# Attention tails transposed with all 128 rows, and the first batch's reciprocals taken from one column named 64 times

## The chip, the cores and the metric

The kernel runs on one core of a Trainium2 chip. The metric is device time in microseconds (us) of that core; lower is better. "Before" is the kernel as it stood, "after" the kernel with the change. The engines are TensorE (PE, with its weight loads shown apart as PEld), VectorE (DVE), ScalarE (ACT), GpSimd (POOL) and the DMA queues (SP and others).

## The reference

Attention with rotary positions feeds two dense blocks. Shapes: batch 4, 8 heads, 576 positions, head size 64; the model width is 512.

```python
def _attn_ref(q, k, v):                       # (4, 8, 576, 64) each
    ...
    q_rot, k_rot = (rotate(q), rotate(k))
    scores = scale * np.matmul(q_rot, k_rot.transpose(0, 1, 3, 2))
    scores = scores - np.max(scores, axis=-1, keepdims=True)
    attn = np.exp(scores)
    attn = attn / (np.sum(attn, axis=-1, keepdims=True) + 1e-09)
    return np.matmul(attn, v).astype(np.float32)

def reference(**kwargs):
    ...
    x = _moe_ref(x=x, **moe_kwargs)           # token mix, relu squared, two products, sigmoid gate
    return _moe2_ref(x=x, **moe2_kwargs)      # relu, normalise, product over positions, gate, product
```

The change touches attention alone: how the matrix of exponentials P (`attn` before the division) is transposed for the product with `v`, and how the row's 1/sum reaches the place where it is multiplied in.

## The kernel before, in words

**Units.** Attention is cut into 72 units, 18 for each batch. Unit m handles 128 query rows of two heads at once, against all 576 keys. 576 is four times 128 and 64 over, so of every nine units the fifth (m mod 9 = 4) is a **tail**: it takes the 64 rows left over of four heads (two pairs). In a tail the rows 0 to 63 of every tile belong to one head of a pair and rows 64 to 127 to the other. The tails are m = 4, 13, 22, 31, 40, 49, 58 and 67; 4 and 13 lie in the first batch (m below 18).

**Steps of a unit**, by the names in the code. `scores` (PE, rows with tile `s`) makes two score tiles, one for each head (in a tail, one for each pair). `top` (DVE, L342) finds the row maxima, once for each score tile. `expo` (ACT, L347) writes P into tile `pf` and the row sums into `sm`; `total` (ACT, L351) adds 1e-9 and `norm` (DVE, L354) takes the reciprocal. `spread` (ACT, L358) copies each reciprocal 64 times wide into tile `rb`. `turn` n = 0, 1, 2 (PE, tile `t`) transposes P in three parts: n = 0 and 1 are four blocks of 128 keys each, n = 2 is the block of left-over keys together with the transposed reciprocals from `rb`. In a tail, `turn` 0 and 1 work on 64 rows at a time, eight blocks each, and `turn` 2 makes eight small products. `take` n (L395) copies the transposed part from PSUM to tile `pt`: n = 0 and 1 on ACT, n = 2 on DVE; in a tail every part goes to two `pt` tiles. `values` (PE, tile `v`, L402) multiplies `pt` with `v`; it follows units 1, 4, 6 and 8 of every nine. `gather` (DVE, L414) multiplies the result by the reciprocals, which stand in chunk 9 of `pt`. In the text t5_2 is part 2 of the turning of unit 5, s6 the scores of unit 6, top 6/0 and exp 6/0 the first of the two `top` and `expo` steps of unit 6.

**Filler.** In the first batch DVE, ACT and POOL also decode the weights (L156 to L174, three DVE steps to a piece: L156, L164, L165) and rotate the next q and k (products L249, sums L257). From unit 19 on PE has products of the finished batch to run between the units (`mk` L498, `mv` L537). After attention come the dense blocks of the second function.

**What sets the order.** A planner (class `Plan`, a list scheduler) is given every step with its engine, an estimated length, what it depends on and a rank, and writes out one fixed order for each engine; the engines then run in that order and wait on semaphores. So a step that is changed in length or in its dependencies can move other steps. The score tiles have two buffers (one unit's worth), so the scores of unit m+1 wait for the exponentials of unit m. The transposed parts have two PSUM slots.

## Time and profile before

| | us |
|---|---|
| median of 3 runs | 777.41 |
| lowest and highest | 776.02 and 779.28 |
| the profiled execution's own time | 777.82 |
| its span, first to last instruction | 776.0 |
| PE busy in the span | 740.8 |
| DVE, ACT busy | 481.0, 463.6 |

The profile is of one execution. A row of the timeline gives the start, the duration, the engine, the line, the operation and its tiles (written <- read), how many instructions were merged, and in brackets how long the engine had been idle and whose end released it. The form in front of the shapes, such as 64*128 or 128*64, is the part of PE's array that the instruction uses, rows by columns. PEld rows start when the weights are loaded. A matmul's own duration is longer than the distance to the next one, since they are pipelined; what a matmul costs a busy PE is the distance from start to start.

### The profile page before, as it was taken

The numbers are of one execution on the slowest core, as the hardware profiler recorded it, in microseconds if no ns is written. First come the engines' busy times: TensorE is split into PE (matmuls) and PEld (weight loads), VectorE is DVE, ScalarE is ACT, GpSimd is POOL, SyncE is SP. The second block draws the span as 40 slices with busy tenths as digits, with TensorE's granted clock in tenths as the row PEclk, the third lists the DMA queues.
The fourth block names the chain that finished last, engine by engine and source line by source line (L and its number), as shares of the span: only waits on it lengthen the run. The fifth ranks groups of instructions, "written<-read, shape, count | busy, mean of one in ns | idle before, by whom it ended". The sixth has DMA issues, their size and how long they took to land.

```text
span 776.0 us, 14283 instructions
## 1 busy us (share of the span) xinstructions
PE 740.8 (95%) x5696; PEld 649.9 (84%) x5696; DVE 481.0 (62%) x881; ACT 463.6 (60%) x1061; POOL 112.2 (14%) x132
## 2 busy tenths in 40 slices
PE   4788889999999999999999999999999999999997
PEld 2555569788888888888888898989989999998997
DVE  5988898888777877687856434246463342545111
ACT  3878898778777878778777644245333322533221
POOL 1432424011211211211111000002020000101000
PEclk9999999999999999999999999999999999999999
DMA  8363540542342442533232175072201212010101
GB/s 294 116 201 122 175 129 20 164 149 99 134 163 85 141 156 88 182 113 126 92 131 70 51 268 210 24 264 57 87 1 62 63 46 77 17 31 1 62 1 62
DMA packets 35268, 84.13 MB, mean 108 GB/s; under 512 B 4545, under 2 KB 10433, under 8 KB 35202
## 3 DMA queue, kind: packets, MB, share of 16 engines
q1 hardware_dynamic: 34658, 82.63, 31.6%
q8 instruction: 45, 0.74, 0.4%
q10 hardware_dynamic: 544, 0.59, 0.3%
q14 instruction: 21, 0.17, 0.1%
HBM read 60.65 MB, written 22.55 MB: 107 GB/s over the span
## 4 chain that ended last, share of the span: by engine, by line
PE 88%; DVE 4%; ACT 3%; DMA 3%; issue 0%; SPq 0%; ACTq 0%
PE mv L537 13%; PE mk L498 11%; PE v L402 11%; PE t L378 9%; PE sp L673 8%; PE r L673 7%; PE u L673 7%; PE hv L737 6%; PE o L673 6%; PE s L330 6%; PE s L338 3%; ACT pf L347 1%; DVE raw L249 1%; DMA wi<-wd 1%; PE s L327 1%; DVE sm L342 1%
## 5 line engine op out<-in xcount | busy, mean ns | idle before, releaser
L342 DVE TENSOR_REDUCE sm<-s 128x1 f32<-128x576 f32 x144 | 107.2, 751 | 36.9 <-PE s L330 30.5
L347 ACT ACTIVATE pf<-s,sm 128x576 f32<-128x576 f32 x144 | 107.0, 745 | 14.1 <-DVE sm L342 13.0
L537 PE MATMUL mv<-kh,wv 128*128 128x288 f32 x512 | 114.1, 305 | 1.2 <-ACT kh L512 1.2
L498 PE MATMUL mk<-x,wk 128*128 128x288 f32 x768 | 110.2, 298 | 0.4 <-ACT rl L505 0.4
L395 ACT COPY pt<-t 128x512 f32<-128x512 f32 (+1 forms) x160 | 84.8, 542 | 34.3 <-PE t L378 32.0
L498 PEld LDWEIGHTS mk<-x,wk 128*128 128x128 f32 x768 | 102.9, 188 | 0.7 <-ACT rl L505 0.6
L378 PE MATMUL t<-ident,pf 128*128 128x128 f32 x512 | 82.5, 284 | 14.0 <-ACT pf L347 14.0
L537 PEld LDWEIGHTS mv<-kh,wv 128*128 128x128 f32 x512 | 85.6, 191 | 5.4 <-issue 3.9
L378 PEld LDWEIGHTS t<-ident,pf 128*128 128x128 f32 x512 | 56.6, 141 | 39.9 <-issue 16.4
L402 PE MATMUL v<-pt,vt 128*64 128x256 f32 (+1 forms) x640 | 87.5, 411 | 0.0
L537 PE MATMUL mv<-kl,wv 128*128 128x288 f32 x256 | 76.5, 299 | 0.6 <-DVE kl L516 0.6
L402 PEld LDWEIGHTS v<-pt,vt 128*64 128x64 f32 x640 | 44.3, 136 | 31.7 <-issue 4.1
L673 PE MATMUL sp<-ws,vn 128*128 128x288 f32 x384 | 53.9, 295 | 0.0
L673 PE MATMUL r<-xr,wr 128*128 128x288 f32 x384 | 52.5, 296 | 1.2 <-ACT vs L543 1.2
L673 PE MATMUL o<-g,wo 128*128 128x288 f32 x384 | 52.9, 296 | 0.5 <-ACT os L796 0.5
L673 PEld LDWEIGHTS r<-xr,wr 128*128 128x128 f32 x384 | 51.7, 188 | 1.8 <-ACT vs L543 1.5
L673 PEld LDWEIGHTS sp<-ws,vn 128*128 128x128 f32 x384 | 52.4, 188 | 0.7
L673 PEld LDWEIGHTS o<-g,wo 128*128 128x128 f32 x384 | 51.7, 188 | 1.4 <-ACT os L796 1.2
L673 PE MATMUL u<-x,wi 128*128 128x288 f32 x384 | 52.0, 296 | 0.0
L673 PEld LDWEIGHTS u<-x,wi 128*128 128x128 f32 x384 | 51.6, 188 | 0.3
L537 PEld LDWEIGHTS mv<-kl,wv 128*128 128x128 f32 x256 | 48.9, 191 | 1.2 <-DVE kl L516 1.2
L249 DVE TENSOR_TENSOR raw<-raw,cst 128x1152 f32<-128x1152 f32 (+1 forms) x34 | 45.6, 1344 | 5.7 <-DMA raw<-kp 4.9
(347 smaller groups left out, 1200.3 us busy)
## 6 DMA issues: line engine op xcount, KB each, us to landing
raw<-kp SPq DMA_DIRECT2D x15, 576.0 KB, 3.8
raw<-qp SPq DMA_DIRECT2D x15, 576.0 KB, 4.3
vt<-vp SPq DMA_DIRECT2D x16, 320.0 KB, 3.8
xd<-xt SPq DMA_DIRECT2D x16, 288.5 KB, 3.2
vd<-vs SPq DMA_DIRECT2D x32, 144.0 KB, 1.8
v<-vd SPq DMA_DIRECT2D x16, 288.0 KB, 2.7
out<-os SPq DMA_DIRECT2D x15, 288.0 KB, 2.1
wi<-wd SPq DMA_DIRECT2D x8, 512.0 KB, 9.1
```

The costliest lines, as they stand in the source:

```text
L249: nc.vector.tensor_tensor(t["raw", k][:, :, z], t["raw", k][:, :, z], cst[:, :, z], op=ALU.mult)
L330: nc.tensor.matmul(ps[j][:, h, :HALF], t[a, 0][r, 128 * c:128 * c + 128], t[b, 1][r, x], **f)
L338: nc.tensor.matmul(o, q[r, 128 * c:min(128 * c + 128, S)], k[r, h * HALF:(h + 1) * HALF], start=True, stop=True)
L342: nc.vector.tensor_reduce(st["sm"][:, 0, j:j + 1], st["s"][j][:, :, :HALF], axis=AX.XY, op=ALU.max, negate=True)
L347: nc.scalar.activation(st["p"][:, j, :].rearrange("p (a b) -> p a b", a=2), st["s"][j][:, :, :HALF], AF.Exp, bias=st["sm"][:, 0, j:j + 1], ...
L378: nc.tensor.transpose(pt[:, c, :], p[:, n, k:k + 128], ident)
L395: nc.scalar.copy(o, x) if eng == "ACT" else nc.vector.tensor_copy(o, x)
L402: nc.tensor.matmul(pv[HEAD[j], z], v[:, 4 * j + c if c < 4 else 8 + j, :], pt[:, 4 * j + c if c < 4 else 8, z], start=c == 0, stop=c == 4)
L498: nc.tensor.matmul(ps[:, :HALF], wk[w][:, c, fc * 128:(fc + 1) * 128], a[:, c, :], start=k == 0, stop=k == 11)
L537: nc.tensor.matmul(xs["v", dc][:, :HALF], wv[w][:, fc, dc * 128:(dc + 1) * 128], a, start=k == 0, stop=k == 23)
L673: nc.tensor.matmul(ps[:, h, :HALF], w, a[:, h * HALF:(h + 1) * HALF], start=m == 0, stop=m == n - 1)
L737: nc.tensor.matmul(ps[:, :FS], x[a][:, d, c:c + 128], wi[w][:, d, FS:], start=k == 0, stop=k == 11)
```

## The change

Three things are changed.

1. A tail's `turn` 0 and 1 transpose all 128 rows at once: four blocks of 128 x 128 each, part 0 for the first pair and part 1 for the second (before, part 0 was the lower 64 rows of both pairs and part 1 the upper 64). Since the two heads' key blocks are offset by 64 keys, the second head's blocks have to be moved up or down by 64 partitions when they are copied. So `take` 0 and 1 of a tail are three copies each instead of two, `take` 2 six instead of two. `turn` 0 now waits for the first exponential alone. The order of chunks in `pt` is changed to fit (ends in chunk 4, second head in chunks 5 to 8).
2. `spread` is left out in the first batch and in all tails. There the reciprocals are turned by a product with the identity whose weights are one column of `sm` named 64 times (two products for a unit, four small ones in a tail). The other units keep the copy and the transpose.
3. The planner's estimates and dependencies for these steps are adapted.

```diff
@@ -360,39 +360,43 @@
         def turn(n, slot):
             pt = st["t", n] = ps_t.tile([128, 4, 128], F32, tag=f"t{slot}", name=f"t{m}_{n}")
             p = st["p"]
-            if tail and n < 2:
+            if tail and n == 2:
                 for u in range(2):
-                    for c in range(4):
-                        k = 64 * n + 128 * c
-                        nc.tensor.transpose(pt.rearrange("p c (h q) -> p (c h) q", h=2)[:, 4 * u + c, :],
-                                            p[HEAD[n], u, k:k + 128], ident[HEAD[n], HEAD[n]])
-            elif tail:
+                    nc.tensor.transpose(pt[0:64, u, :], p[:, u, 512:], ident)
                 for u in range(2):
-                    for k in range(2):
-                        for j, r in enumerate(HEAD):
-                            nc.tensor.matmul(pt[r, u, HEAD[k]], st["r"][r, u, :] if k else p[r, u, 512 - 512 * j:576 - 512 * j],
-                                             ident[r, r], start=True, stop=True)
+                    for j, r in enumerate(HEAD):
+                        nc.tensor.matmul(pt[r, 2 + u, 0:64], st["sm"][r, 3, u:u + 1].to_broadcast([64, 64]), ident[r, r], start=True, stop=True)
             elif n < 2:
                 for c in range(4):
-                    k = 64 * n + 128 * c
+                    k = (0 if tail else 64 * n) + 128 * c
                     nc.tensor.transpose(pt[:, c, :], p[:, n, k:k + 128], ident)
             else:
                 nc.tensor.transpose(pt[:, 0, :], p.rearrange("p a b -> p (a b)")[:, 512:640], ident)
-                nc.tensor.transpose(pt[:, 1, :], st["r"].rearrange("p a b -> p (a b)"), ident)
+                if m >= 18:
+                    nc.tensor.transpose(pt[:, 1, :], st["r"].rearrange("p a b -> p (a b)"), ident)
+                else:
+                    for j, r in enumerate(HEAD):
+                        nc.tensor.matmul(pt[r, 1, :], st["sm"][:, 3, j:j + 1].to_broadcast([128, 64]), ident, start=True, stop=True)
 
         def take(n, eng):
-            for u, d in enumerate(into):
+            for d in into if n == 2 else into[n if tail else 0:][:1]:
                 if "pt" not in d:
                     d["pt"] = at.tile([128, 10, 320], F32, tag=f"pt{d['n'] % PTB}", name=f"pt{d['n']}")
-                o = d["pt"][:, 4 * n:min(4 * n + 4, 10), 256:320]
-                if not tail:
-                    o, x = d["pt"][:, 4 * n:min(4 * n + 4, 10), 128 * part:128 * part + 128], st["t", n]
-                    x = x if n < 2 else x[:, 0:2, :]
-                elif n < 2:
-                    x = st["t", n].rearrange("p c (h q) -> p (c h) q", h=2)[:, 4 * u:4 * u + 4, :]
-                else:
-                    x = st["t", n][:, u, :].rearrange("p (h q) -> p h q", h=2)
-                nc.scalar.copy(o, x) if eng == "ACT" else nc.vector.tensor_copy(o, x)
+            copy = nc.scalar.copy if eng == "ACT" else nc.vector.tensor_copy
+            x, z, (lower, upper) = st["t", n], slice(256, 320), HEAD
+            if not tail:
+                o = into[0]["pt"][:, :, 128 * part:128 * part + 128]
+                copy(o[:, 5 * n:5 * n + 4, :] if n < 2 else o[:, 4:10:5, :], x if n < 2 else x[:, 0:2, :])
+            elif n < 2:
+                o = into[n]["pt"]
+                copy(o[:, 0:4, z], x[:, :, lower])
+                copy(o[upper, 4:8, z], x[lower, :, upper])
+                copy(o[lower, 5:9, z], x[upper, :, upper])
+            else:
+                for u, d in enumerate(into):
+                    copy(d["pt"][lower, 4, z], x[lower, u, lower])
+                    copy(d["pt"][upper, 8, z], x[lower, u, upper])
+                    copy(d["pt"][:, 9, z], x[:, 2 + u, 0:64])
 
         def values(slot):
             pv = duo["v"] = ps_m.tile([128, 512], F32, tag=f"m{slot}", name=f"v{m}")
@@ -400,7 +404,7 @@
             for c in range(5):
                 for j in range(2):
                     nc.tensor.matmul(pv[HEAD[j], z], v[:, 4 * j + c if c < 4 else 8 + j, :],
-                                     pt[:, 4 * j + c if c < 4 else 8, z], start=c == 0, stop=c == 4)
+                                     pt[:, 5 * j + c if c < 4 else 4, z], start=c == 0, stop=c == 4)
 
         def rows(i):
             if i not in xt:
@@ -427,15 +431,16 @@
                              m - 0.5)
         t = add("ACT", 0.2, total, [exps[m, 1]], m - 0.3)
         nm = add("DVE", 0.17, norm, [t], m - 0.3)
-        sp = add("ACT", 0.26, spread, [nm], m - 0.3)
-        ready = [[exps[m, 0], exps[m, 1]] if tail else [exps[m, 0]], [exps[m, 1]], [sp]]
+        sp = nm if tail or m < 18 else add("ACT", 0.3, spread, [nm], m - 0.3)
+        ready = [exps[m, 0], exps[m, 1], sp]
         for n in range(3):
-            turned[m, n] = add("PE", (0.5, 0.5, 0.8)[n] if tail else (0.44, 0.44, 0.22)[n], lambda slot, n=n: turn(n, slot),
-                               ready[n], m + 0.1 * n, take="t", kind="t")
+            turned[m, n] = add("PE", (0.44, 0.44, 0.75 if tail else 0.33 if m < 18 else 0.22)[n], lambda slot, n=n: turn(n, slot),
+                               [ready[n]], m + 0.1 * n, take="t", kind="t")
             eng = ("ACT", "ACT", "DVE")[n]
-            x = add(eng, ((0.68, 0.68, 0.55) if tail else (0.59, 0.59, 0.42))[n], lambda n=n, eng=eng: take(n, eng),
-                    [turned[m, n]] + [y for d in into for y in freed.get(d["n"] - PTB, [])], m - 0.2, give=turned[m, n])
-            for d in into:
+            to = into if n == 2 else into[n if tail else 0:][:1]
+            x = add(eng, (1.13, 1.13, 0.95)[n] if tail else (0.59, 0.59, 0.42)[n], lambda n=n, eng=eng: take(n, eng),
+                    [turned[m, n]] + [y for d in to for y in freed.get(d["n"] - PTB, [])], m - 0.2, give=turned[m, n])
+            for d in to:
                 d["ev"].append(x)
         if part and k != 3 or tail:
             v = add("PE", 2.9 if duo["cols"] > 256 else 2.3, values, duo["ev"] + [vloads[w[0][0]]], m + 0.9, take="m", kind="v")
```

Three places of the order. **DVE around units 5 and 6** (first batch). `raw` are the operands of the rotation, `rot` its result, `I-` pieces of weights, `xt` the attention's result. Before:

```order
L342 TENSOR_REDUCE sm5_380<-s11_379 128x1
L395 COPY pt1_290<-t4_2_405 128x2x64
L395 COPY pt2_386<-t4_2_405 128x2x64
L257 TENSOR_TENSOR rot2_1_437<-raw2_1_264 128x576
L354 RECIPROCAL sm5_380<-sm5_380 128x2
L249 TENSOR_TENSOR raw2_0_269<-raw2_0_269,cst_90 128x1152
L414 TENSOR_TENSOR xt0_276<-v4_426,pt1_290 128x320
L257 TENSOR_TENSOR rot2_0_466<-raw2_0_269 128x576
L342 TENSOR_REDUCE sm6_455<-s12_453 128x1
L395 COPY pt2_386<-t5_2_474 128x2x128
L342 TENSOR_REDUCE sm6_455<-s13_454 128x1
```

After:

```order
L249 TENSOR_TENSOR raw2_0_269<-raw2_0_269,cst_90 128x1152
L354 RECIPROCAL sm5_371<-sm5_371 128x2
L257 TENSOR_TENSOR rot2_0_432<-raw2_0_269 128x576
L156 TENSOR_SCALAR I-435_436<-I-307_308 128x512
L418 TENSOR_TENSOR xt0_276<-v4_414,pt1_288 128x320
L164 TENSOR_SCALAR I-307_308<-I-307_308 128x512
L165 SCALAR_TENSOR_TENSOR I-435_436<-I-435_436,I-307_308 128x512
L389 COPY pt2_392<-t5_2_468 128x2x128
L342 TENSOR_REDUCE sm6_452<-s12_450 128x1
L342 TENSOR_REDUCE sm6_452<-s13_451 128x1
```

The copy of t5_2 and a piece of weights (L156, L164, L165) now stand ahead of the first top of unit 6 (the copies of the tail, two before and six now, stand just ahead of these rows).

**DVE from unit 3 to unit 4** (unit 4 is the first tail). Before:

```order
L342 TENSOR_REDUCE sm3_285<-s7_284 128x1
L156 TENSOR_SCALAR I-311_312<-I-131_132 128x512
L164 TENSOR_SCALAR I-131_132<-I-131_132 128x512
L165 SCALAR_TENSOR_TENSOR I-311_312<-I-311_312,I-131_132 128x512
L234 TENSOR_SCALAR mix4_96<-mix4_96 128x4 x2
L354 RECIPROCAL sm3_285<-sm3_285 128x2
L342 TENSOR_REDUCE sm4_329<-s8_327 128x1
L395 COPY pt1_290<-t3_2_349 128x2x128
L342 TENSOR_REDUCE sm4_329<-s9_328 128x1
```

After:

```order
L342 TENSOR_REDUCE sm3_283<-s7_282 128x1
L156 TENSOR_SCALAR I-310_311<-I-131_132 128x512
L164 TENSOR_SCALAR I-131_132<-I-131_132 128x512
L165 SCALAR_TENSOR_TENSOR I-310_311<-I-310_311,I-131_132 128x512
L249 TENSOR_TENSOR raw2_1_265<-raw2_1_265,cst_90 128x1152
L354 RECIPROCAL sm3_283<-sm3_283 128x2
L342 TENSOR_REDUCE sm4_326<-s8_324 128x1
L389 COPY pt1_288<-t3_2_344 128x2x128
L342 TENSOR_REDUCE sm4_326<-s9_325 128x1
```

A product of the next rotation (L249) has come ahead of the reciprocal of unit 3 and the tops of unit 4, and the two small steps of L234 have left.

**PE, second half of the first tail** (unit 4) to the scores of unit 6 (s12 and s13 are its two score tiles). Before:

```order
L367 MATMUL t4_1_389<-ident_95,pf4_357 128x64 x8
L373 MATMUL t4_2_405<-ident_95,pf4_357 64x64 x2
L373 MATMUL t4_2_405<-ident_95,rb4_401 64x64 x2
L373 MATMUL t4_2_405<-ident_95,pf4_357 64x64 x2
L373 MATMUL t4_2_405<-ident_95,rb4_401 64x64 x2
L378 MATMUL t5_0_421<-ident_95,pf5_415 128x128 x4
L402 MATMUL v4_426<-pt1_290,vt0_134 64x320 x10
L338 MATMUL s12_453<-rot1_1_259,rot1_0_262 128x288
L338 MATMUL s13_454<-rot1_1_259,rot1_0_262 128x288
```

After:

```order
L372 MATMUL t4_1_382<-ident_95,pf4_351 128x128 x4
L365 MATMUL t4_2_396<-ident_95,pf4_351 64x128 x2
L368 MATMUL t4_2_396<-ident_95,sm4_326 64x64 x4
L406 MATMUL v4_414<-pt1_288,vt0_134 64x320 x10
L372 MATMUL t5_0_441<-ident_95,pf5_411 128x128 x4
L338 MATMUL s12_450<-rot1_1_260,rot1_0_263 128x288
L338 MATMUL s13_451<-rot1_1_260,rot1_0_263 128x288
```

The product v4 now comes ahead of t5_0, and the tail's parts are 128 rows deep. Around unit 13 the same happens to v13 and t14_0. Apart from these two places the units' steps on PE stand in the same order up to the first `mk`; of the fillers after it some have moved past a neighbour.

## Rows read from the trace of the kernel before

**Rows 1.** The page, part 2: PE's busy tenths in 40 slices of 19.4 us.

```profile
PE   4788889999999999999999999999999999999997
```

**Rows 2.** Busy time by stage: us, then PE, PEld, DVE, ACT, POOL busy (instructions), clock, DMA.

```profile
8.20:109.00 100.80, 82.28 (x583) 51.79 (x583) 89.27 (x163) 80.89 (x199) 33.30 (x27) 1.00 0.51 167
...
140.00:447.00 307.00, 307.00 (x2626) 263.52 (x2626) 230.88 (x432) 237.21 (x593) 46.01 (x42) 1.00 0.36 121
```

**Rows 3.** PE's waits from 8.2 to 109 us: whom for, total us, times, longest.

```profile
PE t L378 <- ACT pf L347: 14.0, 12, 1.8
...
PE t L381 <- ACT rb L358: 0.8, 1, 0.8
```

**Rows 4.** Groups by line, 8.2 to 109 us: count | busy, mean ns | idle before.

```profile
L358 ACT COPY rb<-sm 128x128 f32<-128x128 f32 x19 | 5.6, 296 | 2.0 <-DVE sm L354 2.0
...
L395 ACT COPY pt<-t 128x256 f32<-128x256 f32 x8 | 2.5, 376 | 0.0
...
L395 DVE COPY pt<-t 128x128 f32<-128x128 f32 x4 | 1.0, 280 | 0.0
```

**Rows 5.** Timeline of one regular pair of units (10 and 11) of the first batch.

```profile
60.70 1.24 PE L338 MATMUL s<-rot,rot 64*128 64x288 f32 x8
...
62.78 0.42 DVE L395 COPY pt<-t 128x256 f32<-128x256 f32 x1
63.05 0.75 ACT L347 ACTIVATE pf<-s,sm 128x576 f32<-128x576 f32 x1
...
64.52 1.50 PE L338 MATMUL s<-rot,rot 64*128 64x288 f32 x8
...
67.28 1.92 PEld L402 LDWEIGHTS v<-pt,vt 128*64 128x64 f32 x18 [0.34 <-ACT pt L395]
...
70.17 1.24 PE L338 MATMUL s<-rot,rot 64*128 64x288 f32 x8
```

**Rows 6.** Timeline around the first tail (unit 4).

```profile
29.34 1.64 DVE L165 SCALAR_TENSOR_TENSOR I-311_312<-I-311_312,I-131_132 128x512 int32<-128x512 int32 x1
...
31.13 0.73 DVE L342 TENSOR_REDUCE sm<-s 128x1 f32<-128x576 f32 x1
...
34.69 1.35 DVE L249 TENSOR_TENSOR raw<-raw,cst 128x1152 f32<-128x1152 f32 x1
...
37.78 0.65 PE L378 MATMUL t<-ident,pf 128*128 128x128 f32 x4 [0.72 <-ACT pf L347]
```

**Rows 7.** Timeline around the second tail (unit 13).

```profile
79.09 0.40 PE L367 MATMUL t<-ident,pf 64*128 64x64 f32 x3 [0.47 <-ACT pf L347]
...
80.40 0.69 DVE L165 SCALAR_TENSOR_TENSOR I-847_848<-I-847_848,I-567_568 128x512 int32<-128x512 int32 x1
...
82.69 0.66 PE L378 MATMUL t<-ident,pf 128*128 128x128 f32 x4 [0.74 <-ACT pf L347]
...
86.11 1.24 PE L338 MATMUL s<-rot,rot 64*128 64x288 f32 x8
```

**Rows 8.** Timeline of PEld while PE is full: scores and a turning between fillers.

```profile
200.02 0.19 PEld L537 LDWEIGHTS mv<-kh,wv 128*128 128x128 f32 x1
200.37 0.30 PEld L330 LDWEIGHTS s<-rh,rh 64*128 64x128 f32 x4 [0.16 <-issue]
...
200.88 0.32 PEld L330 LDWEIGHTS s<-rh,rl 64*128 64x128 f32 x4
201.37 0.42 PEld L378 LDWEIGHTS t<-ident,pf 128*128 128x128 f32 x4 [0.17 <-issue]
...
201.98 0.19 PEld L537 LDWEIGHTS mv<-kh,wv 128*128 128x128 f32 x1
```

**Rows 9.** The same for the end of a tail (unit 40).

```profile
247.62 0.51 PEld L367 LDWEIGHTS t<-ident,pf 64*128 64x128 f32 x7
248.20 0.19 PEld L373 LDWEIGHTS t<-ident,pf 64*64 64x64 f32 x4
...
248.54 0.20 PEld L373 LDWEIGHTS t<-ident,rb 64*64 64x64 f32 x4
```

## The prediction

> **What bounds the kernel now.** I read the utilisation by slices first: PE is at 9 tenths or more from about 140 us to the end and has holes only ahead of that [rows 1]. The stage table says how large they are: from 8.2 to 109 us PE is busy 82.3 of 100.8 us, DVE 89.3 and ACT 80.9, and no engine is full; from 140 to 447 us PE is busy all 307 us and DVE and ACT are not [rows 2]. So there are two different questions. In the first batch the time is a chain that runs around the engines, and only what lies on that chain counts. After 109 us, where PE has the fillers, only PE's own instructions and the gaps between them count.
>
> The chain of the first batch can be read off one regular pair of units [rows 5]. Scores 10 start at 60.70, exponential 10/0 at 63.05, scores 11 at 64.52, then the product v10 (its weight loads go on at 67.28 after a wait of 0.34 for ACT's copy), scores 12 at 70.17. In the first half PE waits for the exponential; such waits sum up to 14.0 us in 12 units, the wait for the widened reciprocal to 0.8 us, once [rows 3]. The copy that widens the reciprocals takes 19 x 0.296 = 5.6 us of ACT in this stretch, with 2.0 us of idle time ahead of it [rows 4], but it stands behind the exponentials, and what waits for it is not on the chain except in that one place.
>
> **The widened copy leaves the first batch and the tails.** 18 copies, 5.3 us of ACT, go in the first batch. On the chain lies at most the one wait of 0.8 us, and there the two small steps of L234 move ahead of the tops of unit 2, which takes some of it back. I count 0, bounds -0.8 and 0 for this alone.
>
> **The reciprocals turned on PE, 16 units of the first batch.** One transpose gives way to two products with 64 columns, each two passes, so four weight loads. The trace has no such row. The nearest are the small products of a tail, 12 starts in 248.54 - 248.20, 0.028 us each [rows 9], and the full transposes, six starts in 201.98 - 201.37, 0.10 each [rows 8]: the four cost 0.11 to 0.41 in place of 0.10, so 0 to 0.3 more; I take 0.15, nearer to the small products, whose column count they share. In the units followed by a product v this lies under the 0.34 us for which v waits for ACT anyway [rows 5], in the others under the wait for the exponential [rows 3]. Cost 0; with the cover gone 16 x 0.15 = 2.4.
>
> **The first tail.** Two waits go: t4_0 no longer waits for the second exponential (0.47 in the twin of unit 13 [rows 7]) and v4 now runs ahead of t5_0, so that t5_0's 0.72 wait for its exponential [rows 6] is filled: -1.2. Against it stands DVE's new order. The piece of weights ends at 29.34 + 1.64 = 30.98; before, top 4/0 followed at 31.13, now a product of 1.35 us comes first [rows 6], so top 4/0 starts near 32.4, 1.3 later. Sum 0.1, counted as 0. The extra copies (ACT six instead of four, DVE six instead of two) are some 2 x 0.3 and 4 x 0.2 us by their likes of 0.376 and 0.280, overlapped [rows 4]; they are hidden by v4, which needs the last of them only at its end.
>
> **Unit 6.** This is the clearest loss. In the order before, top 6/0 runs as soon as its scores are there. Now the copy of t5_2 stands ahead of it, and PE makes t5_2 after scores 6. In the regular pair that copy starts 62.78 - 60.70 = 2.08 us after the scores and takes 0.42 [rows 5]; with a t5_2 that is 0.2 longer, top 6/0 can start at 2.7 and, at 0.73 us for a top [rows 6], the exponential at 3.4 instead of 63.05 - 60.70 = 2.35. So +1.1 on the chain; scores 7 and all that follows wait for it. Queued behind on DVE are top 6/1 and the next piece of weights.
>
> **The second tail.** The same two waits go, 0.47 and 0.74 [rows 7], and here no product comes ahead of the tops. The six copies of t13_2 now stand ahead of top 14/1, but scores 15 start so late before (86.11 [rows 7]) that its exponential is there in time. -1.2, less 0.2 for the longer part 2: -1.0.
>
> **Six tails after 109 us, where PE is full.** Instructions first. Before, 16 transposes of 64 rows at about 0.06 (seven in 0.51 us, one taking 0.14) and 16 small products at 0.028 [rows 9]: 1.44 us. After, 8 + 2 transposes at 0.10 [rows 8] and 8 small products at 0.028: 1.24. So -0.2 each, -1.2 for six. Then the gaps. When the form changes, PE loses time between starts: from 128*128 to 64*128, 200.37 - 200.02 = 0.35 us where like follows like in 0.10; back again, the twelfth score starts at 201.07 (0.064 apart) and the next transpose at 201.37, 0.30 instead of 0.064 [rows 8]. That is 0.24 for each change; inside the tail, from 64*128 to 64*64, the last transpose starts at 247.99 and the first small product at 248.20, 0.21 instead of 0.06, so 0.15 [rows 9]. Before, a tail's part 0, its neighbour scores and part 1 shared the form 64*128. After, parts 0 and 1 are 128*128 and the scores are not, and part 2 has two forms of its own. Counted through the two orders of PE from the first `mk` to the last v, there are 141 changes of form before and 155 after. 14 x 0.2 = 2.8. Sum for this stretch -1.2 + 2.8 = +1.6.
>
> The Trainium skill, "TensorEngine Tiling (Array Packing)", section "Key Properties", states that a change of tiling mode, not of the tile alone, drains the TensorE. It gives no figure; by that rule every one of the 14 costs something, and the trace agrees with its 0.15 to 0.24 us.
>
> **Sum.** 0 + 0 + 0 + 1.1 - 1.0 + 1.6 = +1.7. Against the profiled execution (777.82, span 776.0) that is 779.5; the median of the three runs, 777.41, lies 0.41 lower, so the forecast is 777.41 + 1.7 = 779.1.
>
> **Rivals.** (B) The gaps at a change of form cost nothing here, since matmuls already queued run on through them. For it speaks that PE's row is called busy all the time [rows 2]; against it that the starts themselves stand apart [rows 8]. Then the later tails give their 1.2: 777.41 + 0.1 - 1.2 = 776.3. (C) ACT sets the pace of the first batch after all. Its 5.3 us of copies and the 2.0 idle ahead of them go, less the tails' added copies, 4 x 0.3: 6.1 us earlier at the first filler, and with +1.6 behind it 777.41 - 6.1 + 1.6 = 772.9. Against it: only 0.8 us of PE's waits name that copy [rows 3], and ACT is busy 80% [rows 2]. (D) DVE becomes late, slower than before: the place is the order ahead of tops 4/0, 6/0 and 14/1. One DVE step of L165 took 1.64 us [rows 6], another of the same shape 0.69 [rows 7], so DVE steps can be held up by 0.95; if the moved product and sum around unit 4 are held up by half of that (0.5 each) and the six copies hold back exponential 14/1 so that the second tail's 1.0 isn't gained, the first batch loses 1.1 at unit 6 and 1.0 there, 2.1, and if the thinner instructions bring nothing the later stretch loses 2.8: 777.41 + 2.1 + 2.8 = 782.3. It decides once the two losses come to more than 3.9.
>
> **How the numbers follow.** Half a per cent, 3.9 us, is about what a measurement of this kernel tells from no change: 773.5 to 781.3. Forecast 0.45, B 0.22, C 0.12, D 0.21. Faster 0.12 (C); slower 0.21 (D) and a little of the forecast's upper end, 0.24; same the other 0.64. The range leaves out most of C and the far end of D: 774.5 to 783.0.
>
> **What would show it.** Between 109 us and the last v the span from the first `mk` to the end of attention should be 1 to 3 us longer, with more PEld gaps of 0.15 to 0.24 at the tails; if it is shorter, B. The first `mk` should start within 1.5 us of 109; near 103 it is C, past 111 D. Top 6/0 should start some 2.7 us after scores 6, and scores 15 should come 1 us earlier relative to unit 13 than before. The four products of the reciprocals should stand 0.03 to 0.1 us apart; if each took several times that, the first batch's cover of 0.34 us is gone and the sum wrong by 2.4 or more. The forecast also falls if the order of fillers on DVE and ACT, which moved at many more places than I walked through, makes other tops late.

## The result and the profile after

The kernel after takes 783.45 us (median of 5, 781.80 to 784.41) against 777.41: a ratio of 1.0067, 95% interval 1.0051 to 1.0083. By the medians that is 6.0 us more where 1.7 were forecast, 0.45 above the top of the range; by the ratio it is 5.2 us more (777.41 x 1.0067 = 782.6), which lies inside it. The profiled execution after took 784.18 us, its span 782.4 (before 776.0).

The starts of the same pieces of work in the two traces show where the 6.4 us of span went.

| stretch | before | after | difference |
|---|---|---|---|
| scores 0 to scores 6 | 33.01 | 32.62 | -0.39 |
| scores 6 to v6 | 6.06 | 9.25 | +3.19 |
| v6 to v10 | 19.49 | 19.72 | +0.23 |
| v10 to scores 15 | 19.35 | 18.13 | -1.22 |
| scores 15 to v17 | 15.94 | 16.95 | +1.01 |
| v17 to v71 (late tails) | 344.01 | 346.67 | +2.66 |
| v71 to the first `r` | 61.08 | 61.80 | +0.72 |
| from there to the end | 268.86 | 269.04 | +0.18 |

First the stage table after, the columns as in [rows 2].

```profile
8.20:109.00 100.80, 86.03 (x591) 53.43 (x592) 87.63 (x169) 76.76 (x180) 33.48 (x27) 0.98 0.50 163
...
140.00:447.00 307.00, 305.37 (x2531) 260.15 (x2528) 235.89 (x452) 240.10 (x596) 47.38 (x42) 1.00 0.38 122
```

ACT lost 4.1 us of work in the first batch (80.89 to 76.76) and nothing came of it. PE is busy 3.75 us longer, and the clock, the last column but two, is 0.98 where it was 1.00. After 140 us PE now has holes of 1.6 us, where it had none. PE's waits from 8.2 to 109 us, as in [rows 3]:

```profile
PE t L372 <- ACT pf L347: 12.9, 11, 2.6
...
PE t L379 <- DVE sm L354: 1.6, 2, 0.8
```

The wait for the exponential is shorter in sum (14.0 before), but the longest one is now 2.6 us, where it was 1.8. It stands at unit 6:

```profile
40.82 1.51 DVE L156 TENSOR_SCALAR I-435_436<-I-307_308 128x512 f32<-128x512 f32 x1
40.84 1.24 PE L338 MATMUL s<-rot,rot 64*128 64x288 f32 x8
...
44.04 1.42 DVE L342 TENSOR_REDUCE sm<-s 128x1 f32<-128x576 f32 x2
...
44.82 0.74 ACT L347 ACTIVATE pf<-s,sm 128x576 f32<-128x576 f32 x1 [1.05 <-DVE sm L342]
...
45.71 0.66 PE L372 MATMUL t<-ident,pf 128*128 128x128 f32 x4 [2.56 <-ACT pf L347]
...
48.36 1.11 PE L372 MATMUL t<-ident,pf 128*128 128x128 f32 x4
...
50.09 2.96 PE L406 MATMUL v<-pt,vt 128*64 128x320 f32 x20
```

The row of t6_0 before, for comparison:

```profile
44.45 0.66 PE L378 MATMUL t<-ident,pf 128*128 128x128 f32 x4 [1.19 <-ACT pf L347]
```

Top 6/0 starts 3.2 us after scores 6 (2.7 forecast), and PE waits 2.56 us where it waited 1.19. Then comes something that the forecast didn't have: t6_1, four transposes (the row at 48.36), takes 1.11 us instead of 0.66. The windows of PE there (us, busy, granted clock, DMA) show why:

```profile
46.00:48.00 2.00, 2.00 (x12) 0.69 0.75 202
48.00:50.00 2.00, 2.00 (x11) 0.50 0.32 127
50.00:52.00 2.00, 2.00 (x18) 0.96 0.62 242
```

PE runs at 0.50 of its clock, 1.2 instead of 2.4 GHz, behind a pause. Before, the window of the first batch shows 1.00 [rows 2]. From the start of t6_0 to v6 it takes 4.38 us, in place of 2.82.

The regular pair of units 10 and 11, the rows of [rows 5] and some more:

```profile
63.32 1.24 PE L338 MATMUL s<-rot,rot 64*128 64x288 f32 x8
...
64.88 0.14 PEld L374 LDWEIGHTS t<-ident,pf 128*128 128x128 f32 x1
65.18 0.20 PEld L379 LDWEIGHTS t<-ident,sm 128*64 128x64 f32 x4 [0.17 <-issue]
...
65.67 0.42 DVE L389 COPY pt<-t 128x256 f32<-128x256 f32 x1 [0.32 <-PE t L379]
...
66.80 0.74 ACT L347 ACTIVATE pf<-s,sm 128x576 f32<-128x576 f32 x1 [0.29 <-DVE sm L342]
...
67.14 1.77 PE L338 MATMUL s<-rot,rot 64*128 64x288 f32 x8
...
67.68 0.78 PEld L338 LDWEIGHTS s<-rot,rot 64*128 64x128 f32 x6 [0.24 <-ACT pf L347]
...
70.17 1.92 PEld L406 LDWEIGHTS v<-pt,vt 128*64 128x64 f32 x18 [0.23 <-ACT pt L389]
...
73.06 1.24 PE L338 MATMUL s<-rot,rot 64*128 64x288 f32 x8
```

From scores 10 to scores 12 it is 9.74 us, 9.47 before. DVE's copy of t9_2 starts 2.35 us after the scores (2.08 before), and it now waits for PE. Behind it stands top 10/1, behind that the second exponential of unit 10, which now has a wait of 0.29, and scores 11 are held up in their second tile by 0.24. Before, the second exponential of unit 10 had no wait:

```profile
63.91 0.74 ACT L347 ACTIVATE pf<-s,sm 128x576 f32<-128x576 f32 x1
```

From 8.2 to 102 us exponentials wait for a top 16 times after (15.2 us in all) and 3 times before (9.0 us in all); the longest single wait, 8.0 us, is the same in both.

Last, a late tail (unit 31, PEld, as in [rows 9]) and two of PE's new waits further on:

```profile
192.40 0.42 PEld L372 LDWEIGHTS t<-ident,pf 128*128 128x128 f32 x4 [0.17 <-issue]
192.78 0.22 PEld L365 LDWEIGHTS t<-ident,pf 128*64 128x64 f32 x2
193.20 0.31 PEld L368 LDWEIGHTS t<-ident,sm 64*64 64x64 f32 x8 [0.20 <-issue]
...
367.48 0.66 PE L372 MATMUL t<-ident,pf 128*128 128x128 f32 x4 [0.76 <-ACT pf L347]
...
408.50 0.87 PE L406 MATMUL v<-pt,vt 128*64 128x256 f32 x6 [0.86 <-ACT pt L389]
```

The eight small products start some 0.3 us after the second of the two transposes, the change of form showing as 0.20 of "issue". The first of the two waits is for an exponential that stands behind the second half of a tail's six copies and two fillers on ACT; before the second wait ACT's copy stands behind a weight step:

```profile
407.31 0.68 ACT L160 ACTIVATE I-5096_5097<-I-5096_5097 128x512 int32<-128x512 uint32 x1 [3.20 <-DMA I-5096_5097<-w_out]
407.89 0.56 ACT L389 COPY pt<-t 128x512 f32<-128x512 f32 x1
```

That step waits 3.20 us for its load. Between 109 us and the last v PE waits 1.9 us by name, 0.5 before.

### The profile page after: what moved, and what is told of

Same layout as the page of the kernel before. It is cut to its first block, busy times and chain, and to the rows that moved or that the text cites. A ratio compares the mean times of both kernels' runs of the same rounds, so it can differ in the third digit from the quotient of the medians.

```text
span 782.4 us, 14169 instructions
## 1 busy us (share of the span) xinstructions
PE 748.9 (96%) x5632; PEld 652.9 (83%) x5632; DVE 483.4 (62%) x913; ACT 466.0 (60%) x1053; POOL 114.2 (15%) x132
## 4 chain that ended last, share of the span: by engine, by line
PE 86%; DVE 4%; DMA 4%; ACT 3%; issue 1%; SPq 0%; ACTq 0%; DVEq 0%
PE mv L542 13%; PE mk L503 10%; PE v L406 9%; PE t L372 9%; PE sp L678 8%; PE r L678 7%; PE u L678 7%; PE hv L742 6%; PE o L678 6%; PE s L330 6%; PE s L338 3%; PE s L327 1%; ACT pf L347 1%; DVE sm L342 1%; DMA wi<-wd 1%; DMA I-5096_5097<-w_out 1%
## 5 line engine op out<-in xcount | busy, mean ns | idle before, releaser
L503 PE MATMUL mk<-x,wk 128*128 128x288 f32 x768 | 113.2, 300 | 0.3 <-ACT rl L510 0.3
L372 PE MATMUL t<-ident,pf 128*128 128x128 f32 x576 | 92.8, 284 | 13.7 <-ACT pf L347 13.7
L372 PEld LDWEIGHTS t<-ident,pf 128*128 128x128 f32 x576 | 64.2, 141 | 41.5 <-issue 18.2
L389 ACT COPY pt<-t 128x512 f32<-128x512 f32 x128 | 74.4, 582 | 37.4 <-PE t L372 36.4
L249 DVE TENSOR_TENSOR raw<-raw,cst 128x1152 f32<-128x1152 f32 (+1 forms) x34 | 44.6, 1313 | 5.8 <-DMA raw<-kp 4.9
```

The costliest lines, as they stand in the source:

```text
L249: nc.vector.tensor_tensor(t["raw", k][:, :, z], t["raw", k][:, :, z], cst[:, :, z], op=ALU.mult)
L372: nc.tensor.transpose(pt[:, c, :], p[:, n, k:k + 128], ident)
L389: copy(o[:, 5 * n:5 * n + 4, :] if n < 2 else o[:, 4:10:5, :], x if n < 2 else x[:, 0:2, :])
L503: nc.tensor.matmul(ps[:, :HALF], wk[w][:, c, fc * 128:(fc + 1) * 128], a[:, c, :], start=k == 0, stop=k == 11)
```

## The experiments

Twelve kernels ran, in three groups; each group has its own runs of the kernel before on the same chip. The ratios come from the executions of the two kernels and need not equal the quotient of the medians. Executions of one kernel lie some us apart, and their mean granted clock goes with it: of the 87 executions of before in the three groups, the 12 that took 781.5 us or more had 0.988 to 0.990, the other 75 had 0.992 or more and took 780.2 or less. A trace shows one execution alone.

| kernel | median us | before, same group | ratio, 95% interval |
|---|---|---|---|
| e_order | 787.50 | 778.19 | 1.0107 (1.0076 to 1.0138) |
| e_unit6 | 785.12 | 778.19 | 1.0073 (1.0047 to 1.0099) |
| e_wait | 780.03 | 778.19 | 1.0015 (0.9993 to 1.0036) |
| e_recip | 783.43 | 778.19 | 1.0045 (1.0024 to 1.0065) |
| w_recip | 781.11 | 778.49 | 1.0025 (1.0007 to 1.0043) |
| w_before | 779.01 | 778.49 | 1.0001 (0.9985 to 1.0018) |
| e_first | 780.55 | 778.49 | 1.0034 (1.0021 to 1.0048) |
| e_late | 782.76 | 778.49 | 1.0056 (1.0034 to 1.0078) |
| sw_recip | 778.96 | 778.26 | 0.9996 (0.9979 to 1.0012) |
| sw_first | 777.76 | 778.26 | 0.9993 (0.9981 to 1.0006) |
| sw_after | 779.78 | 778.26 | 1.0020 (1.0011 to 1.0029) |
| f_form | 797.70 | 778.26 | 1.0249 (1.0232 to 1.0266) |

Two theories stood at the start. Theory 1: the loss is the planner's new order, which makes top 6/0 late, and the clock that falls behind the wait. Theory 2: it is the new instructions.

**e_order: the new instructions in the old order.** The planner keeps the lengths and dependencies of before, and a step in place of `spread` that issues nothing where the column is named. (The kernels of the experiments carry switches for the parts of the change; here and in e_recip the code is shown with the switches put in.)

```diff
-        sp = nm if tail or m < 18 else add("ACT", 0.3, spread, [nm], m - 0.3)
-        ready = [exps[m, 0], exps[m, 1], sp]
+        sp = add("ACT", 0.26, spread, [nm], m - 0.3)
+        ready = [[exps[m, 0], exps[m, 1]] if tail else [exps[m, 0]], [exps[m, 1]], [sp]]
...
-            turned[m, n] = add("PE", (0.44, 0.44, 0.75 if tail else 0.33 if m < 18 else 0.22)[n], ...
+            turned[m, n] = add("PE", (0.5, 0.5, 0.8)[n] if tail else (0.44, 0.44, 0.22)[n], ...
```

> All new instructions of the change (tails turned with 128 rows, reciprocals from a named column, extra copies), but every engine's order is that of the kernel before: the planner keeps the old lengths and dependencies. Theory 1, the loss comes from the new order: the wait ahead of t6_0 is 1.2 us again (not 2.6), the clock stays at 1.0 from 46 to 52 us, the first mk starts within 0.7 us of 109, and only the later tails' 6 x 0.24 = 1.5 us remain: 778.5 to 779.5. Theory 2, the loss comes from the new instructions: 782 or more, whatever the order.

It came out slower still, 787.5. Two of Theory 1's signs are there: the wait ahead of t6_0 is 0.93 us, and the clock is 1.00 from 46 to 52 us. But the first `mk` starts at 114.3, not within 0.7 us of 109. From v17 to v71 it takes 349.56 us, 5.55 more than before and 2.9 more than after. PE's waits from 109 to 460 us:

```profile
PE t L389 <- ACT pf L348: 2.1, 4, 1.2
PE t L391 <- ACT pt L406: 1.5, 2, 1.3
PE v L431 <- ACT pt L406: 0.7, 1, 0.7
```

All are for ACT, 4.3 us; before has 0.5 there. The tails' additional copies stand ahead of exponentials and other copies in an order that was made for shorter ones. So Theory 1 falls in its main part: the new order isn't what costs most. It seems to save some of what the new instructions cost: every execution of e_order took 785.45 us or more, every one of after 784.41 or less, though the intervals of the two ratios overlap.

**e_unit6: after, with DVE's order at unit 6 repaired.** Three steps are moved in the list that the planner has made.

```diff
+        for a, b in [(("top", 6, 0), ("scale", 4)), (("take", 5, 2), ("gather", 4)), (("top", 6, 1), ("take", 5, 2))]:
+            r = row[at[a].eng]
+            r.remove(at[a])
+            r.insert(r.index(at[b]) + 1, at[a])
```

> The kernel after, with one repair on DVE: around unit 6 top 6/0, the copy of t5_2 and top 6/1 come ahead of the two steps L164 and L165 of the weight piece, and top 6/0 ahead of the gather of v4; nothing else moves. Theory 1: top 6/0 starts 1.5 us after scores 6 in place of 3.2, the wait ahead of t6_0 falls from 2.56 to about 0.9 us, the granted clock stays at 1.0 from 46 to 52 us, v6 starts 2.8 us earlier and about that much is left at the end: 780.6. Theory 2: v6 comes earlier, but the wait comes back in a later unit of the first batch, and the time stays within 1 us of 783.4.

```profile
42.66 1.24 PE L357 MATMUL s<-rot,rot 64*128 64x288 f32 x8
...
44.05 0.74 DVE L361 TENSOR_REDUCE sm<-s 128x1 f32<-128x576 f32 x1
...
45.23 0.53 ACT L520 ACTIVATE mt<-xt,mix 128x288 f32<-128x288 f32 x1 [1.32 <-DVE xt L461]
...
46.13 0.74 ACT L366 ACTIVATE pf<-s,sm 128x576 f32<-128x576 f32 x1
...
47.02 0.66 PE L407 MATMUL t<-ident,pf 128*128 128x128 f32 x4 [2.05 <-ACT pf L366]
```

Top 6/0 comes 1.39 us after the scores, as meant, but the exponential only 2.1 us behind its start. ACT has a filler (`mt`) ahead of it, and that waits 1.32 us for the gather, which I had put behind the top. PE still waits 2.05 us, the clock is at 0.63 and 0.52 from 48 to 52 us (and at 0.72 and 0.50 from 34 to 38, ahead of the repair), and the time doesn't fall. The repair moved the wait from DVE's order to ACT's: a miss.

**e_wait: before, with that one wait added.**

```diff
+        for a, b in [(("top", 6, 0), ("take", 5, 2))]:
+            r = row[at[a].eng]
+            r.remove(at[a])
+            r.insert(r.index(at[b]) + 1, at[a])
```

> The kernel before, with one swap on DVE: top 6/0 runs behind the copy of t5_2. It adds to the kernel before the one wait that is suspected. Top 6/0 starts 2.4 us after scores 6 in place of 1.3, and PE's wait ahead of t6_0 grows from 1.2 to 2.3 us. Theory 1, a wait of that length costs more than itself since the granted clock falls behind it: clock near 0.5 for 3 to 5 us, v6 2.5 to 2.8 us later, the time 779.5 to 780.2. Rival: the clock in the kernel after fell for another reason; here it stays at 1.0 and the time grows by the wait alone, 1.1 us at most: 778.5.

The row of t6_0 in the timeline, and two windows of PE (us, busy, granted clock, DMA):

```profile
45.60 0.66 PE L407 MATMUL t<-ident,pf 128*128 128x128 f32 x4 [2.05 <-ACT pf L366]
```

```profile
46.00:48.00 2.00, 2.00 (x16) 1.00 0.36 146
...
82.00:84.00 2.00, 1.60 (x21) 0.50 0.34 136
```

The wait is there, v8 starts 1.0 us later, and behind it the clock is at 1.00. In this execution it falls at 81 us, around the second tail, where nothing was changed. So the fall isn't bound to that one wait; the wait alone costs 1 us. The median, 780.03, would suit Theory 1, but the trace doesn't, and the time can't be told from that of before.

**e_recip: only the reciprocals of the first batch.** The old tails, the old order.

```diff
-                nc.tensor.transpose(pt[:, 1, :], st["r"].rearrange("p a b -> p (a b)"), ident)
+                if m >= 18:
+                    nc.tensor.transpose(pt[:, 1, :], st["r"].rearrange("p a b -> p (a b)"), ident)
+                else:
+                    for j, r in enumerate(HEAD):
+                        nc.tensor.matmul(pt[r, 1, :], st["sm"][:, 3, j:j + 1].to_broadcast([128, 64]), ident, start=True, stop=True)
```

> The kernel before in its own order, with the reciprocals of the 16 units of the first batch that are not tails turned from one named column, and their widened copies left out; tails unchanged. Theory 1: the products cost nothing on the chain (777.4, at most 0.8 less for the one wait that goes). Theory 2: they cost 16 x 0.15 = 2.4 us, 779.8. If ACT set the pace, 5.3 us of copies fewer would show as a first mk 3 us or more earlier.

This small edit alone costs 0.45%, 3.5 us, more than either theory gave, and the first `mk` starts at 112.3, no earlier than before, so ACT didn't set the pace. In its trace a pair of units is 0.27 us longer, with the same three rows as in the pair shown of after, and from 80 to 88 us the clock is low:

```profile
82.00:84.00 2.00, 1.60 (x22) 0.50 0.12 46
84.00:86.00 2.00, 1.97 (x8) 0.50 0.80 250
```

Two new theories, then. Theory 3: the products cost nothing, and the loss is the clock, which falls where PE pauses. Theory 4: the products cost time on the chain.

**w_recip and w_before: PE's pauses filled.** Eight transposes of the identity, overwritten at once, stand ahead of part 0 in nine units of the first batch, in e_recip and in before.

```diff
             p = st["p"]
+            if n == 0 and m in (3, 4, 6, 8, 10, 12, 13, 15, 17):
+                for c in range(8):
+                    nc.tensor.transpose(pt[:, c % 4, :], ident, ident)
```

> The kernel e_recip (reciprocals of the first batch from a named column, order of before) with eight additional transposes of the identity ahead of part 0 of units 3, 4, 6, 8, 10, 12, 13, 15 and 17, where PE waits 0.9 to 1.2 us for the exponential; what they write is overwritten at once. They take 0.8 us of each such wait and no more. Theory 3, the products cost nothing on the chain and e_recip lost its time to stretches of half clock behind PE's pauses: no such stretch between 20 and 110 us, v17 starts within 0.5 us of before's 102.05, 778 to 779. Theory 4, the loss lies in the products themselves: still 782 or more.

> The kernel before with the same eight additional transposes ahead of part 0 of nine units of the first batch. Theory 3: the mean granted clock is 0.997 or more in every run, the runs between 782 and 784 that the kernel before shows go away, the median is 777.3 to 778. Theory 4: the pauses have no bearing on the clock, the runs spread as before, or the additional transposes stand on the chain and cost up to 9 x 0.3 = 2.7 us: 779 to 781.

The windows of w_recip in the same place as those of e_recip:

```profile
82.00:84.00 2.00, 1.22 (x26) 1.00 0.61 233
84.00:86.00 2.00, 1.77 (x14) 1.00 0.33 68
```

In both traces the clock is at 1.00 from 20 to 110 us. In w_before v17 stands where it stood (101.90, before 102.05), so the additional transposes cost nothing on the chain. The ratio is 1.0001; the median of 779.01 is above the 777.3 to 778 that Theory 3 gave and at the lower end of Theory 4's 779 to 781, though v17 shows no time on the chain. The executions lie between 777.76 and 780.04, those of before in this group between 776.07 and 783.15; but only 4 of the 35 of before lie above 782 there, so that 12 without one could be chance. w_recip is 1.6 us faster than e_recip by the ratios (0.0045 - 0.0025), and yet 2.0 slower than before. The intervals of the two ratios overlap; the mean clocks speak for a difference, 0.996 to 1.000 in the executions of w_recip and 0.993 to 0.996 in those of e_recip. Its v17 is 2.1 us later than that of w_before, their first scores set equal, and this grows by about 0.27 a pair. So both theories hold a part: some 2 us were the products, which the trace shows, and some 1.6, an estimate from the ratios, the clock.

The Trainium skill, "TensorE: Matmul & The Clock Gate", Part 1, states that the throttled clock is the default, which activity releases, and that how many matmuls of a kernel run throttled at its start varies from run to run. The traces agree with the first: the clock is at 1.00 in both traces in which the pauses are filled. No run here shows the second; in the middle of the kernel the low stretches stand at different places, at 46 us after and at 81 in e_wait, beside either of the two tails.

**e_first and e_late: the change in one half each.** `new` selects the new turning and copying of a tail, `named` the named column, `old` the estimates and dependencies of before.

```diff
         duo = into[0]
+        new, named, old = tail and (m < 18), m < 18, m >= 18
```

```diff
         duo = into[0]
+        new, named, old = tail and (m >= 18), tail and m >= 18, m < 18
```

> The change in the first batch alone (tails 4 and 13 and all reciprocals), the later tails and their planning as before. By the traces read so far the first batch of the kernel after is 1.1 us longer without the clock and 1.7 longer by one stretch of half clock: 780.5 to 781. If the later order moves by itself, more.

> The change in the six later tails alone; the first batch as before. By the traces read so far the stretch from v17 to v71 is 2.7 us longer in the kernel after, 1.4 of it from waits of PE for ACT and 1.3 from the instructions and changes of form: 780 to 781. If the later tails were only as dear as the instructions, 778.2 + 1.3 = 779.5.

e_first takes 780.55, as expected; its v17 is 2.6 us later than before, with the clock at 0.63 and 0.52 from 46 to 50 us, and the rest of the kernel isn't longer. e_late is dearer than expected, but its own stretch from v17 to v71 is only 1.8 us longer (345.80); v17 itself came 4.7 us late, in a first batch whose order and instructions are those of before, with the clock at half in two places (35 to 42 and 83 to 90 us). Its time therefore says little on the tails; its trace does.

That left the mechanism of the 2 us. Theory 5: part 2 ends 0.26 us later, and DVE's copy of it stands between the two tops. Theory 6: the products lie on PE's own path.

**sw_recip: w_recip with DVE's copy of part 2 behind both tops.**

```diff
+        r = row["DVE"]
+        for m in range(1, 18):
+            a, b = at["take", m - 1, 2], at["top", m, 1]
+            if r.index(at["top", m, 0]) < r.index(a) < r.index(b):
+                r.remove(a)
+                r.insert(r.index(b) + 1, a)
```

> The kernel w_recip (reciprocals of the first batch from a named column, additional transposes in PE's pauses), with one swap on DVE in each unit of the first batch where it occurs: the copy of the third part t_2 of the unit before runs behind both tops and no longer between them. Theory 5, the products cost time because part 2 ends 0.26 us later, DVE's copy of it stands between the two tops, and so the second exponential comes late by 0.29 us, once in a pair of units: with the swap the second exponential follows the first without a wait, v17 starts within 0.5 us of w_before's 101.9, and the time is 779.0 (w_recip: 781.1). Theory 6, the products lie on PE's own path: v17 stays 2 us later and the time at 781.

Unit 10 again:

```profile
60.85 1.42 DVE L367 TENSOR_REDUCE sm<-s 128x1 f32<-128x576 f32 x2
...
62.19 0.41 DVE L433 COPY pt<-t 128x256 f32<-128x256 f32 x1
62.65 0.75 ACT L372 ACTIVATE pf<-s,sm 128x576 f32<-128x576 f32 x1
62.66 1.09 PE L392 MATMUL t<-ident 128*128 128x128 f32 x8 [0.78 <-DVE pt L433]
```

ACT's waits for the tops from 8.2 to 102 us, first in w_recip, then in sw_recip (3 times, 8.8 us, in w_before):

```profile
ACT pf L348 <- DVE sm L343: 13.1, 15, 8.0
...
ACT pf L372 <- DVE sm L367: 9.3, 3, 7.7
```

The two tops of unit 10 run as one row, the second exponential has no wait, v17 is 0.5 us from that of w_before (101.90), and the time is that of before. Theory 5 is shown, and Theory 6 is out: PE makes the same products. The swap has a price of its own: the copy comes later, so the additional transposes of unit 10 wait 0.78 us for it where they waited 0.53 in w_recip, and this one pair takes 9.93 us (9.75 in w_recip), while that of units 8 and 9 takes 9.35 (9.74). The same swap in the kernel before wasn't run. There exponentials wait for tops 3 times in all, so it has little to win.

**sw_first and sw_after: the repairs together.** e_first and the whole kernel after, with the three moves of e_unit6, the loop of sw_recip and the eight transposes of w_recip, no other edit:

```diff
+        for a, b in [(("top", 6, 0), ("scale", 4)), (("take", 5, 2), ("gather", 4)), (("top", 6, 1), ("take", 5, 2))]:
...
+        for m in range(1, 18):
...
+                    nc.tensor.transpose(pt[:, c % 4, :], ident, ident)
```

> The kernel e_first (the change in the first batch alone) with the repairs found so far: the order of e_unit6 at unit 6, the copy of part 2 behind both tops, additional transposes in PE's pauses. If the three causes add up (1.1 for unit 6, 2.1 for the copies between the tops, up to 1.7 for a stretch of half clock, and 1 each gained by the two tails), the first batch ends 1 to 2 us earlier than in the kernel before: 777 to 778. If the gain of the tails is taken up by later waits: 778.5 to 779.5.

> The whole kernel after with the same three repairs of its first batch; the later tails as they are. The later tails keep their 2.7 us: 780 to 781.5. If the first batch's causes were misread, it stays at 783.

sw_first took 777.76, in the expected range, and sw_after 0.2 less than expected. But sw_first's v17 starts at 102.5, no earlier than before (102.05). The tails gain (0.6 us up to scores 6, 1.5 from v10 to scores 15), but from scores 6 to v6 it still takes 8.04 us where before takes 6.06: the three moves of e_unit6 don't mend unit 6, where ACT's `mt` again waits for the gather, here 2.27 us. Its interval holds 1, so no version beats the kernel before measurably. sw_after is at 1.0020 where the kernel after is at 1.0067: with the repairs 3.7 of 5.2 us are given back. PE's waits in it from 109 to 452 us:

```profile
PE t L416 <- ACT pf L372: 0.8, 1, 0.8
PE t L418 <- ACT pt L433: 0.3, 1, 0.3
```

From v17 to v71 it is only 1.1 us longer than before (345.11), although the order there is that of the kernel after (2.66 longer). So not all that was given back is due to the first batch: 1.6 us of the difference between the two traces lies where no edit was made. In its profile one low stretch was left, 0.50 from 46 to 48 us: there the additional transposes themselves waited 1.86 us for a free slot and left the pause unfilled.

**f_form: the cost of a change of form.** Before, with a small product between two transposes, in 48 late units.

```diff
                 nc.tensor.transpose(pt[:, 0, :], p.rearrange("p a b -> p (a b)")[:, 512:640], ident)
+                if m >= 18:
+                    nc.tensor.matmul(pt[0:64, 2, 0:64], ident[0:64, 0:64], ident[0:64, 0:64], start=True, stop=True)
```

> The kernel before with one additional small product (64*64, identity times identity, into an unused part of the t tile) between the two transposes of part 2 in each of the 48 units from 18 on that are not tails: 96 changes of form more on a PE that is full. If a change of form costs 0.15 to 0.24 us there, and the product itself 0.06: 48 x 0.06 + 96 x 0.2 = 22 us, 800 in all. Rival B of the prediction, that the changes are free: 3 us, 781.

```profile
205.95 0.14 PEld L391 LDWEIGHTS t<-ident,pf 128*128 128x128 f32 x1
206.25 0.19 PEld L393 LDWEIGHTS t<-ident 64*64 64x64 f32 x2 [0.17 <-issue]
206.51 0.14 PEld L395 LDWEIGHTS t<-ident,rb 128*128 128x128 f32 x1
```

It takes 797.70 us, 2.3 less than expected. The two transposes start 0.56 us apart in place of 0.10. From v17 to v71 it is 18.55 us longer, 0.39 for each unit; less 0.06 for the product that leaves 0.16 for a change. The rule of the Trainium skill that the prediction cited, "TensorEngine Tiling (Array Packing)", "Key Properties", agrees with it, and rival B is out.

## Why the prediction was right and wrong

**The sign was right, the size was not**: 1.7 us were forecast and 5.2 to 6.0 measured, at the top of a range whose upper part stood there for rival D. Terms that I had put at 0 or had too small make up most of it. Step by step:

- *Widened copy, 0:* right. ACT's 4.1 us less moved nothing; the first `mk` starts at 110.3, within 1.5 us of 109. Rival C is out.
- *Reciprocals, 0, hidden:* the step that failed. I sized the product and then asked only what on PE covers it: the 0.34 wait ahead of v and the wait for the exponential. Half of that holds: PE's waits shrink (1.19 to 0.93, 0.34 to 0.23). But I didn't follow who waits for the *end* of part 2. DVE's copy of it stands between the two tops, as the order of before shows for units 4 and 6, and through it the delay reaches the chain once a pair, 0.27 us, about 2 us in all; w_recip and sw_recip show it. The term also lacked the change of form ahead of the products, which I counted for the late tails: from the transposed keys to the first product it is 0.30 us from load to load, before 0.11. My own figure for "with the cover gone", 2.4, was near the 2 us by luck, since it is a sum over PE's time in 16 units and not this path.
- *First tail, 0:* measured -0.39. The late top that I had counted against it came as forecast (32.3).
- *Unit 6, +1.1:* right mechanism, wrong size: +3.19. The wait grew by 1.37 (top 3.2 us after the scores, since a step of L156 ahead of it took 1.51 us instead of 0.42), the longer t5_2 is 0.26, and from t6_0 to v6 it is 1.56 more, some 0.2 of it the longer t6_2 and the rest, by this estimate, the half clock, which no step had. That the order of DVE alone could be mended, as I thought, e_unit6 disproved.
- *Second tail, -1.0:* measured -1.22 up to scores 15, and scores 15 come 1.06 us earlier relative to scores 13, as forecast; then 1.0 is lost up to v17. The six copies ahead of top 14/1 do hold up exponential 14/1, by 0.17 us, as in rival D, and the pairs' 0.27 comes on top; the rest I can't assign.
- *Late tails, +1.6:* from v17 to v71 it is +2.66 after, +1.1 in sw_after, +1.8 in e_late, +5.55 in e_order. PE's idle time from 110 to 460 us grew by 1.4, 0.4, 1.7 and 4.0 of that, so 1.3, 0.7, 0.1 and 1.6 are left for instructions and changes of form. All four kernels have the new tails, so that remainder scatters from trace to trace; with the 0.16 of f_form for a change my term would be 14 x 0.16 - 1.2 = 1.0, which suits it. What I had put nothing in for are the waits: ACT's longer copies make exponentials or `pt` late here and there, and how much depends on the order. One of them, the 0.86 at 408.50, isn't theirs: the weight step ahead of it waited 3.20 us for its load after, 0.46 in sw_after, whose order is the same there. By the sign that I had named, from the first `mk` to the last v, it is 4.1 us longer after, past the 1 to 3 that I gave.
- *After attention, 0:* +0.7 in that profile. I have no cause for it; e_first shows 0.2 there and e_recip 1.2, and neither changes anything behind unit 17, so single traces scatter by as much there.

Rival D came nearest in time (782.3), with unit 6 and the tops behind the tail's copies as its places; but its main places weren't the ones that cost. What stays open is in which executions the clock falls, at which of the two tails, and how much of the late stretch is the tails' and how much scatter.

## What to carry to other kernels

Before an addition is called hidden, follow its end as well as its start: the first step on another engine that reads the result, and what stands behind that step in its fixed order. In a stretch where the chain runs around the engines, a copy that nobody is in a hurry for belongs behind the steps that the chain needs. And a stretch in which the matmul engine pauses can lose its clock; there a change is judged by the trace with the granted clock beside it, since a few us may be the clock's alone.

## What the runs showed of the hardware

I had not expected the granted clock to fall to 0.50 in the middle of a kernel whose PE is busy 96% of the span. In the profiled executions it fell in the first batch, around units 4 to 7 or 13 to 14, in seven of the twelve experiments and after, at different places in kernels that don't differ there. In the trace of before it stayed at 1.00 there and fell once behind attention (0.52 and 0.63 from 470 to 474 us). With eight transposes of the identity in nine of the pauses it stayed at 1.00 in the first batch in four of five kernels; over all 59 executions of these five the mean clock was 0.994 or more, over the 87 of before 0.988 or more. The four weight loads of the two products from a named column take 0.20 us together, little more than the 0.14 of one full transpose, but the part ends 0.27 us later: most of that is the change of form ahead of them (0.30 us from load to load in place of 0.11).
